# A new order table for the steps and the first loads of a windowed-attention and highway kernel

## The chip, the cores and the metric

The kernel runs on one core of a Trainium2 chip. The metric is the device time of one execution in microseconds (us). The engines of a core run side by side, each through its own program in order: PE (TensorE, matrix multiplies and transposes), DVE (VectorE), ACT (ScalarE), POOL (GpSimd) and SP (SyncE). They wait for one another on semaphores. Most loads are issued by POOL, the stores by SP.

## The reference

For each of 4 x 8 heads, 768 queries of 64 elements attend to the first 4 keys (the sinks) and to the last 128 keys. The result, 3072 tokens of 512 elements, goes through a highway layer.

```python
keep = (pos[None, :] < n_sink) | ((rel >= 0) & (rel < window))
a = softmax(where(keep, scale * q @ k.T, -1e9))
x = a @ v                                   # heads side by side: 3072 x 512
H = maximum(x @ w_h, 0.0)
T = 1.0 / (1.0 + exp(-(x @ w_t + b_t)))
out = T * H + (1.0 - T) * x
```

## The kernel before

The 3072 tokens are cut into 24 blocks of 128, six to a batch entry. The keys and values are cut into chunks that lie 64 rows off, so that a block needs chunks n-1, n and n+1. For each block n the work is a chain of small steps, and one step is one function. The steps are named as in the table ORDER (line 594):

- On PE, **Tq:n** and **Tk:n** (line 272) transpose the block's queries and the chunk's keys, eight small transposes each. From block 3 on they sit inside S ("hosted", line 528): S:n transposes the queries of a later block and the keys of another. Then ACT copies the result out of PSUM, **tq:n** and **tk:n** (line 283). The variants tqV and tkV do the copy on DVE.
- **S:n** (line 540, PE) makes the scores; **x0_:n** and **x1_:n** (line 339, ACT) take the exponentials of four heads each; **m0_:n** and **m1_:n** (line 347, DVE) multiply by the window's mask.
- **sk:n** (line 300, PE) and **es:n** (line 309, ACT) do the scores and exponentials of the sinks. They use a sink matrix that POOL copies for later batch entries (line 289, with tk:6, tk:12 and tk:18), and the sinks' values, a product with a small mask bm: fc:0 and fd:0 on DVE for the first batch entry, POOL for the others. POOL makes bm itself, with the two selections at lines 194 and 197.
- **A:n** (lines 354 and 366, PE) multiplies with the values. It needs value chunks n-1 to n+1, both masked halves of the exponentials, and, from block 1, the sinks. Placing A:n also places the loads of queries n+8 and of keys and values n+9 in POOL's program (do_A, line 560).
- **xh:n** (lines 390 and 396, DVE) divides by the sum; **X:n** (line 406, PE) transposes the result; **xT:n** (line 415) copies it on ACT, or xTV:n on DVE.
- The highway part: **Mh:n** and **Mt:n** (PE, lines 435 and 421) multiply with the two weights; **u:n** (ACT) takes a tanh; **d:n**, **e:n** and **o:n** (DVE) combine them; o:n also issues the store on SP.
- **wA:n** is a spare matmul of zeros into the buffer of A:n. It does no work for the result.

The scores have two PSUM buffers, the output of A one pair of banks (so A:n+1 waits for the copy xT:n), and sk, Mh and Mt share two buffers. Five xh and three each of u, d and e can be alive.

The order is written out by hand: the table lists all steps, and each engine runs its own steps in the table's order (line 629). Whatever an engine cannot yet do holds everything behind it on that engine. The loads of the first blocks stand in a list of their own at the head of POOL's program (lines 186 to 214). The very first loads (q0, k0, k1, v0, v1) come over SP and ACT in 32 bits.

Of the kernel before, what the change touches and what calls it, by code (L numbers as in the profile page):

```python
# [20 lines left out]
def kernel(  # L21
# [21 lines left out]
    B, H, S, D = q.shape  # L43
# [37 lines left out]
    def chunk_parts(n):  # L81
        b, c = divmod(n, NSC)
        if c:
            return [(slice(0, P), b, c * P - HP)]
        return ([(slice(0, HP), b - 1, S - HP)] if b else []) + ([(slice(HP, P), b, 0)] if b < B else [])

    def load_q(n):
        b, c = divmod(n, NSC)
        qsd = sd_pool.tile([P, H, D], FP16, tag="qsd", name="qsd")
        nc.gpsimd.dma_start(out=qsd, in_=q[b, :, c * P:(c + 1) * P, :].transpose([1, 0, 2]))  # L90
        q_sd[n] = qsd

    def load_k(n):
        ksd = sd_pool.tile([P, H, D], FP16, tag="ksd", name="ksd")
        for rows, b, s0 in chunk_parts(n):
            nr = rows.stop - rows.start
            nc.gpsimd.dma_start(out=ksd[rows], in_=k[b, :, s0:s0 + nr, :].transpose([1, 0, 2]))  # L97
        k_sd[n] = ksd

    def load_v(n):  # L100
        vt = v_ring[n % NV][:, 0:H * 65].rearrange("p (h e) -> p h e", e=65)
        for rows, b, s0 in chunk_parts(n):
            nr = rows.stop - rows.start
            nc.gpsimd.dma_start(out=vt[rows, :, 0:D], in_=v[b, :, s0:s0 + nr, :].transpose([1, 0, 2]))  # L104
# [12 lines left out]
    wh_sb = const.tile([P, NOC, DM], FP16, tag="wh")  # L117
# [25 lines left out]
    def load_f32(kind, n, eng):  # L143
        t = kf_first if (kind, n) == ("k", 0) else const.tile([P, H, D], FP32, tag=f"{kind}f{n}",
                                                              name=f"{kind}f{n}")
        src = {"q": q, "k": k, "v": v}[kind]
        for rows, b, s0 in ([(slice(0, P), 0, n * P)] if kind == "q" else chunk_parts(n)):
            nr = rows.stop - rows.start
            eng.dma_start(out=t[rows], in_=src[b, :, s0:s0 + nr, :].transpose([1, 0, 2]))
        {"q": q_sd, "k": k_sd, "v": vf_of}[kind][n] = t  # L150
# [6 lines left out]
    def tri(t, rows, lo, hi, base, step, cm):  # L157
        nc.gpsimd.affine_select(
            out=t[rows, lo:hi], in_=t[rows, lo:hi], compare_op=ALU.is_ge, fill=0.0,
            base=base, pattern=[[step, hi - lo]], channel_multiplier=cm)  # L160
# [6 lines left out]
    def load_w(w, sb):  # L167
        nc.gpsimd.dma_start(out=sb, in_=w.rearrange("(kc p) of -> p kc of", p=P))

    with tc.manual_schedule(engines={ENG.Pool, ENG.SP}):  # L170
        load_f32("q", 0, nc.sync)
        load_f32("k", 0, nc.scalar)
        load_f32("k", 1, nc.sync)
        load_f32("v", 0, nc.scalar)
        load_f32("v", 1, nc.sync)
        nc.sync.dma_start(out=bt32, in_=moe_b_t.unsqueeze(0))
        for b in range(B):
            nc.sync.dma_start(out=vs_dn[b], in_=v[b, :, 0:NSINK, :])
        nc.gpsimd.affine_select(
            out=ident, in_=ident, compare_op=ALU.is_equal, fill=0.0,  # L180
            base=0, pattern=[[-1, P]], channel_multiplier=1)
        tri(mask, slice(0, HP), 0, P, HP - 1, -1, 1)
        tri(mask, slice(HP, P), 0, P, 0, 1, -1)
        tri(mask, slice(0, HP), P, EW, 0, 1, -1)
        tri(mask, slice(HP, P), P, EW, -1, -1, 1)
        load_q(3)
        load_k(2)
        load_q(4)
        load_q(1)
        load_k(3)  # L190
        load_q(2)
        load_v(2)
        load_k(5)
        nc.gpsimd.affine_select(
            out=bm, in_=bm, compare_op=ALU.is_ge, fill=0.0,
            base=0, pattern=[[-NSINK, H]], channel_multiplier=1)
        nc.gpsimd.affine_select(
            out=bm, in_=bm, compare_op=ALU.is_ge, fill=0.0,
            base=NSINK - 1, pattern=[[NSINK, H]], channel_multiplier=-1)
        load_k(4)  # L200
        load_v(3)
        load_w(moe_w_h, wh_sb)
        load_q(5)
        load_k(6)
        load_w(moe_w_t, wt_sb)
        load_v(4)
        load_q(6)
        load_k(7)
        load_v(5)
        load_k(8)  # L210
        load_q(7)
        load_v(6)
        load_v(8)
        load_v(7)
# [378 lines left out]
    }  # L593
    ORDER = """
    mz0_:0 ma:0 na:0 Tq:0 na:1 Tk:0 tq:0 mz1_:0 tk:0 ma:1 wA:0 wA:0 Tk:1 mc:0 cv:0 tk:1 fa:0
    wA:0 wA:0 wA:0 S:0 cv:1 x0_:0 fb:0 x1_:0 wA:0 wA:0 wA:0 wA:0 Tq:3 m0_:0 tq:3 wA:0 Tk:2 m1_:0
    tk:2 fc:0 fd:0 wA:0 wA:0 wA:0 wA:0 wA:0 Tq:1 A:0 tq:1 S:1 xh:0 sk:1 x0_:1 x1_:1 Tq:2 m0_:1
    X:0 sk:3 xTV:0 es:1 Tk:3 m1_:1 tq:2 tk:3 wA:1 A:1 es:3 S:2 xh:1 x0_:2 x1_:2 Tk:4 m0_:2 sk:2
    tkV:4 X:1 es:2 m1_:2 S:3 xT:1 A:2 x0_:3 Mh:1 x1_:3 xh:2 tq:4 d:1 X:2 Mh:0 xT:2 m0_:3 tk:5
    m1_:3 Mh:2 d:0 S:4 d:2 Mt:0 x0_:4 x1_:4 m0_:4 A:3 u:0 m1_:4 Mt:1 tq:5 xh:3 tk:6 sk:4 e:0 u:1  # L600
    S:5 es:4 o:0 X:3 x0_:5 sk:5 xTV:3 e:1 A:4 x1_:5 m0_:5 Mt:2 tq:6 xh:4 tk:7 es:5 m1_:5 X:4 u:2
    S:6 xTV:4 o:1 A:5 x0_:6 e:2 Mh:3 x1_:6 xh:5 Mh:4 tq:7 m0_:6 tk:8 m1_:6 X:5 S:7 d:3 xT:5 d:4
    A:6 x0_:7 o:2 Mh:5 x1_:7 xh:6 Mt:3 tq:8 d:5 tk:9 X:6 m0_:7 u:3 Mt:5 m1_:7 xT:6 e:3 sk:7 u:5
    o:3 Tq:9 es:7 Mt:6 e:5 tq:9 o:5 u:6 S:8 A:7 x0_:8 Mh:6 x1_:8 xh:7 tq:10 m0_:8 X:7 tk:10
    m1_:8 sk:9 xT:7 d:6 S:9 es:9 e:6 A:8 x0_:9 o:6 Mt:7 x1_:9 xh:8 tq:11 Mt:4 m0_:9 tk:11 m1_:9
    u:7 X:8 u:4 S:10 xTV:8 e:4 A:9 x0_:10 o:4 Mh:8 x1_:10 xh:9 Mh:7 tq:12 m0_:10 tk:12 m1_:10
    X:9 S:11 xT:9 d:8 A:10 d:7 x0_:11 sk:11 e:7 x1_:11 Mt:8 xh:10 es:11 tq:13 Mh:9 o:7 tk:13 u:8
    m0_:11 X:10 S:12 xT:10 m1_:11 d:9 A:11 x0_:12 e:8 Mt:9 x1_:12 xh:11 tq:14 Mh:10 m0_:12 tk:14
    m1_:12 u:9 X:11 d:10 S:13 xT:11 o:8 A:12 x0_:13 e:9 sk:13 x1_:13 xh:12 Mt:10 es:13 m0_:13
    tq:15 Mh:11 m1_:13 tk:15 o:9 u:10 X:12 S:14 d:11 xT:12 e:10 A:13 x0_:14 o:10 Mt:11 x1_:14  # L610
    xh:13 tq:16 Mh:12 tk:16 m0_:14 u:11 m1_:14 X:13 S:15 d:12 xT:13 e:11 A:14 x0_:15 o:11 sk:15
    x1_:15 Mt:12 xh:14 es:15 tq:17 m0_:15 Mh:13 tk:17 m1_:15 u:12 X:14 d:13 S:16 xT:14 e:12 A:15
    x0_:16 o:12 Mt:13 x1_:16 xh:15 tq:18 Mh:14 m0_:16 tk:18 m1_:16 u:13 X:15 d:14 S:17 xT:15
    e:13 A:16 x0_:17 o:13 sk:17 x1_:17 Mt:14 xh:16 es:17 tq:19 m0_:17 Mh:15 tk:19 m1_:17 u:14
    X:16 d:15 S:18 xT:16 e:14 A:17 x0_:18 o:14 Mt:15 x1_:18 xh:17 tq:20 Mh:16 m0_:18 tk:20
    m1_:18 u:15 X:17 d:16 S:19 xT:17 e:15 A:18 x0_:19 o:15 sk:19 x1_:19 Mt:16 xh:18 es:19 m0_:19
    tq:21 Mh:17 m1_:19 tk:21 u:16 X:18 d:17 S:20 xT:18 e:16 A:19 x0_:20 o:16 Mt:17 x1_:20 xh:19
    tq:22 Mh:18 m0_:20 u:17 m1_:20 tk:22 sk:21 d:18 X:19 es:21 S:21 xTV:19 e:17 A:20 x0_:21 o:17
    Mt:18 x1_:21 xh:20 tq:23 Mh:19 m0_:21 u:18 m1_:21 tk:23 X:20 d:19 sk:23 xT:20 S:22 e:18
    es:23 A:21 x1_:22 o:18 Mt:19 x0_:22 xh:21 tk:24 m0_:22 X:21 xT:21 m1_:22 S:23 u:19 A:22  # L620
    x0_:23 e:19 Mh:20 xh:22 x1_:23 Mh:21 d:20 m0_:23 X:22 Mt:21 xT:22 m1_:23 d:21 A:23 o:19 u:21
    e:21 Mh:22 xh:23 Mt:22 d:22 o:21 X:23 u:22 Mt:20 xT:23 e:22 Tb:23 o:22 u:20 Ta:23 ub:23 e:20
    Ha:23 ua:23 o:20 Hb:23 da:23 db:23 ea:23 eb:23 pa:23 pb:23
    """

    with tc.manual_schedule(engines={ENG.PE, ENG.DVE, ENG.Activation, ENG.SP, ENG.Pool}):
# [40 lines left out]
```

The softmax here doesn't subtract the row's maximum and nothing guards it: scores larger than these inputs give would overflow.

## Time and profile before

| | |
|---|---|
| median of 3 runs | 124.67 us (123.35 to 126.68) |
| the profiled execution's own time | 122.54 us |
| its span, first to last instruction | 120.5 us |
| PE busy | 109.2 us (91%) |
| DVE busy | 103.1 us (86%) |
| ACT busy | 92.7 us (77%) |
| POOL busy | 73.7 us (61%) |
| granted TensorE clock | 0.996 |

The profile is of one execution. "L426" is line 426 of the kernel. In a timeline, a line gives start, duration, engine, line, operation, result and source, how many instructions are merged, and in brackets how long the engine was idle before it and what ended that. In a table of stretches, each number is the busy time of an engine in the stretch, with its count of instructions. A load on POOL shows the time POOL needs to issue it; when the data lands is a separate number of the transfer view. PE instructions overlap, so the step times in this text are the distances between starts.

### The profile page before, as it was taken

To read this page: it belongs to the slowest core of one execution; us is meant where nothing else is said; L and a number is where in the kernel's file an instruction comes from. 1 tells how busy PE (TensorE), PEld (TensorE's weight loads), DVE (VectorE), ACT (ScalarE), POOL (GpSimd) and SP (SyncE) were. 2 spreads that over 40 slices of the span, in tenths; PEclk is the share of its full clock that TensorE was granted. 3 is DMA by queue.
4 is the path that set the end of the run, shared out by engine and by line. 5 is a ranking of instruction groups with operands and counts; after the bars stand their busy time and mean duration, and the time that the engine had idled before them with its cause. 6 is when DMAs were issued, how large, how long until landed. Compare 5 with 4: busy or idle time off the path is not lost.

```text
span 120.5 us, 4964 instructions
## 1 busy us (share of the span) xinstructions
PE 109.2 (91%) x2105; PEld 66.0 (55%) x2105; DVE 103.1 (86%) x237; ACT 92.7 (77%) x155; POOL 73.7 (61%) x97
## 2 busy tenths in 40 slices
PE   5999696999999999997999999989999999999920
PEld 1443565456666466565567656645775676545610
DVE  6889456769999979998889999899998999899990
ACT  2258478949987879998799999979999979961610
POOL 5999996958799999999899999760000000000000
PEclk9999999999999999999999999999999999999998
DMA  2999999999999999999999999999122202202242
GB/s 67 218 172 151 151 172 170 189 155 146 134 196 203 170 235 193 152 201 195 165 201 109 191 200 202 200 163 234 29 92 87 95 5 87 87 5 87 87 174 87
DMA packets 79847, 17.65 MB, mean 146 GB/s; under 512 B 75601, under 2 KB 76881, under 8 KB 79826
## 3 DMA queue, kind: packets, MB, share of 16 engines
q0 software_dynamic: 71888, 9.97, 131.5%
q1 hardware_dynamic: 6882, 7.11, 18.8%
q10 hardware_dynamic: 1056, 0.26, 1.3%
q8 instruction: 16, 0.26, 0.9%
q14 instruction: 5, 0.04, 0.1%
HBM read 21.01 MB, written 6.29 MB: 227 GB/s over the span
## 4 chain that ended last, share of the span: by engine, by line
PE 57%; DMA 18%; POOL 7%; DVE 6%; issue 4%; ACT 4%; DVEq 0%; ACTq 0%; POOLq 0%
DMA qsd<-in_q_dram 18%; PE tps L426 11%; PE hps L439 11%; PE av L368 6%; PE av L379 5%; PE sps L336 4%; PE sps L323 4%; PE sps L280 4%; PE sk L305 3%; PE tps L424 3%; ACT e L341 3%; PE av L385 3%; PE av L412 3%; POOL qsd L90 2%; POOL ksd L97 2%
## 5 line engine op out<-in xcount | busy, mean ns | idle before, releaser
L341 ACT ACTIVATE e<-sps,ebias 128x768 f16<-128x768 f32 x48 | 40.7, 898 | 8.4 <-PE sps L336 7.0
L349 DVE TENSOR_TENSOR e<-e,mask 128x768 f16<-128x768 f16 x48 | 24.8, 550 | 2.4 <-ACT e L341 2.4
L285 ACT COPY t<-sps 128x512 f16<-128x512 f16 x45 | 24.4, 586 | 1.5 <-PE sps L280 1.5
L104 POOL DMA_DIRECT2D v<-in_v_dram x26 | 22.4, 861 | 3.6 <-DVE e L349 1.0
L426 PE MATMUL tps<-wt_sb,xT 128*128 128x512 f16 x92 | 23.6, 379 | 0.0
L439 PE MATMUL hps<-wh_sb,xT 128*128 128x512 f16 x92 | 23.0, 379 | 0.0
L97 POOL DMA_DIRECT2D ksd<-in_k_dram x26 | 22.5, 874 | 0.2
L90 POOL DMA_DIRECT2D qsd<-in_q_dram x23 | 21.5, 936 | 1.3 <-DMA qsd<-in_q_dram 0.8
L451 DVE SCALAR_TENSOR_TENSOR ee<-u,dd 128x512 f16<-128x512 f16 x23 | 17.2, 748 | 0.9 <-ACT u L432 0.7
L398 DVE TENSOR_TENSOR xh<-av,rec 128x512 f16<-128x512 f32 x24 | 16.6, 691 | 0.8
L432 ACT ACTIVATE u<-tps 128x512 f16<-128x512 f32 x23 | 13.8, 602 | 4.3 <-PE tps L426 4.2
L445 DVE SCALAR_TENSOR_TENSOR dd<-hps,xh 128x512 f16<-128x512 f32 x23 | 15.6, 687 | 1.5 <-PE hps L439 1.1
L457 DVE SCALAR_TENSOR_TENSOR otok<-xh,ee 128x512 f32<-128x512 f16 x23 | 15.8, 689 | 0.6
L439 PEld LDWEIGHTS <-xT 128*128 128x128 f16 x92 | 8.9, 98 | 9.2 <-ACT xT L417 0.2
L426 PEld LDWEIGHTS <-xT 128*128 128x128 f16 x92 | 9.0, 98 | 8.6
L417 ACT COPY xT<-av 128x512 f16<-128x512 f16 x19 | 11.2, 587 | 2.1 <-PE av L412 2.0
L323 PE MATMUL sps<-t,t 64*128 64x128 f16 x192 | 11.9, 217 | 0.1
L368 PEld LDWEIGHTS <-e 64*64 64x64 f16 x384 | 9.3, 107 | 3.0 <-issue 1.2
L368 PE MATMUL av<-v,e 64*64 64x66 f16 x384 | 10.8, 193 | 0.2 <-DVE xT L417 0.2
L379 PE MATMUL av<-v,e 128*128 128x66 f16 x192 | 10.4, 195 | 0.0
L393 DVE RECIPROCAL rec<-av 128x8 f32<-128x8 f32 x24 | 4.9, 204 | 5.9 <-PE av L385 4.4
L336 PE MATMUL sps<-t,t 64*64 64x64 f16 x384 | 8.0, 198 | 1.4 <-issue 1.4
(79 smaller groups left out, 140.4 us busy)
## 6 DMA issues: line engine op xcount, KB each, us to landing
out_dram<-otok SPq DMA_DIRECT2D x23, 256.0 KB, 5.1
qsd<-in_q_dram POOLq DMA_DIRECT2D x23, 128.0 KB, 6.7
ksd<-in_k_dram POOLq DMA_DIRECT2D x19, 128.0 KB, 6.6
v<-in_v_dram POOLq DMA_DIRECT2D x19, 128.0 KB, 6.8
wh_sb<-in_moe_w_h_dram POOLq DMA_DIRECT2D x1, 512.0 KB, 7.0
wt_sb<-in_moe_w_t_dram POOLq DMA_DIRECT2D x1, 512.0 KB, 8.3
ksd<-in_k_dram POOLq DMA_DIRECT2D x7, 64.0 KB, 6.6
v<-in_v_dram POOLq DMA_DIRECT2D x7, 64.0 KB, 6.1
```

The lines of the kernel that those rows point to most:

```text
L90: nc.gpsimd.dma_start(out=qsd, in_=q[b, :, c * P:(c + 1) * P, :].transpose([1, 0, 2]))
L97: nc.gpsimd.dma_start(out=ksd[rows], in_=k[b, :, s0:s0 + nr, :].transpose([1, 0, 2]))
L104: nc.gpsimd.dma_start(out=vt[rows, :, 0:D], in_=v[b, :, s0:s0 + nr, :].transpose([1, 0, 2]))
L285: (eng or nc.scalar.copy)(out=t.rearrange("p a (h b) -> p h a b", b=HP), in_=t_view(s_tile(n, g), isinstance(n, tuple) and n[1:] in F32_T))
L323: nc.tensor.matmul(sps[:, hh, hl * EW:hl * EW + P], lhsT=kT[n][rows, hp, :], rhs=qT[n][rows, hp, :], start=True, stop=True)
L341: nc.scalar.activation(out=e.rearrange("p a b c -> p a (b c)"), in_=s_tile(n, g)[:, :, 0:2 * EW], func=AF.Exp, bias=ebias, scale=SCALE)
L349: nc.vector.tensor_tensor(out=ev, in0=ev, in1=m.unsqueeze(1).to_broadcast([P, 4, EW]), op=ALU.mult)
L368: nc.tensor.matmul(av[part, h // 4, h % 4, 0:_AVN], lhsT=e_at(n, h)[src, P:EW], rhs=vt[src, 65 * h:65 * h + _AVN], start=(h % 4 == 0), sto ...
L398: nc.vector.tensor_tensor(out=xh.rearrange("p (h d) -> p h d", d=D), in0=av_of.pop(n)[:, :, 0:D], in1=rec_of.pop(n).unsqueeze(2).to_broadc ...
L426: nc.tensor.matmul(tps, lhsT=xT[:, kc, :], rhs=wt_sb[:, kc, :], start=False, stop=(kc == NOC - 1))
L439: nc.tensor.matmul(hps, lhsT=xT[:, kc, :], rhs=wh_sb[:, kc, :], start=(kc == 0), stop=(kc == NOC - 1))
L451: nc.vector.scalar_tensor_tensor(out=ee, in0=u_of.pop(n), scalar=1.0, in1=dd_of.pop(n), op0=ALU.add, op1=ALU.mult)
```

## The change

Nothing is added to or taken from what is computed. The first loads in POOL's program come in another order, and the two selections that make bm come after the load of q5. In the table, the steps of blocks 0 to 13 and of the last five blocks come in another order. In the middle the rows are the same, shifted. Block 1's keys and queries are transposed ahead of those of block 3; the first highway step comes after A:2 for block 0, and Mh:1 only before S:8. Three copies of transposes are on DVE (tkV:3, tqV:2, tqV:3) where there was one (tkV:4), and the copies xTV are at blocks 1, 4, 6, 12 and 20 (0, 3, 4, 8 and 19 before). There are 20 spares where there were 16.

```diff
@@ -183,32 +183,32 @@
-        load_q(3)
         load_k(2)
-        load_q(4)
         load_q(1)
         load_k(3)
         load_q(2)
+        load_k(5)
+        load_k(4)
+        load_q(4)
+        load_k(6)
+        load_v(3)
+        load_q(3)
         load_v(2)
-        load_k(5)
+        load_v(4)
+        load_w(moe_w_h, wh_sb)
+        load_q(5)
         nc.gpsimd.affine_select(
             out=bm, in_=bm, compare_op=ALU.is_ge, fill=0.0,
             base=0, pattern=[[-NSINK, H]], channel_multiplier=1)
         nc.gpsimd.affine_select(
             out=bm, in_=bm, compare_op=ALU.is_ge, fill=0.0,
             base=NSINK - 1, pattern=[[NSINK, H]], channel_multiplier=-1)
-        load_k(4)
-        load_v(3)
-        load_w(moe_w_h, wh_sb)
-        load_q(5)
-        load_k(6)
         load_w(moe_w_t, wt_sb)
-        load_v(4)
         load_q(6)
         load_k(7)
         load_v(5)
+        load_q(7)
         load_k(8)
-        load_q(7)
         load_v(6)
@@ -593,34 +593,34 @@
-    wA:0 wA:0 wA:0 S:0 cv:1 x0_:0 fb:0 x1_:0 wA:0 wA:0 wA:0 wA:0 Tq:3 m0_:0 tq:3 wA:0 Tk:2 m1_:0
-    tk:2 fc:0 fd:0 wA:0 wA:0 wA:0 wA:0 wA:0 Tq:1 A:0 tq:1 S:1 xh:0 sk:1 x0_:1 x1_:1 Tq:2 m0_:1
-    X:0 sk:3 xTV:0 es:1 Tk:3 m1_:1 tq:2 tk:3 wA:1 A:1 es:3 S:2 xh:1 x0_:2 x1_:2 Tk:4 m0_:2 sk:2
-    tkV:4 X:1 es:2 m1_:2 S:3 xT:1 A:2 x0_:3 Mh:1 x1_:3 xh:2 tq:4 d:1 X:2 Mh:0 xT:2 m0_:3 tk:5
-    m1_:3 Mh:2 d:0 S:4 d:2 Mt:0 x0_:4 x1_:4 m0_:4 A:3 u:0 m1_:4 Mt:1 tq:5 xh:3 tk:6 sk:4 e:0 u:1
...
+    wA:0 wA:0 wA:0 S:0 cv:1 x0_:0 fb:0 x1_:0 wA:0 wA:0 wA:0 wA:0 Tk:2 m0_:0 tk:2 wA:0 Tq:1 m1_:0
+    tq:1 wA:0 wA:0 wA:0 S:1 x0_:1 x1_:1 wA:0 wA:0 wA:0 wA:0 Tk:3 m0_:1 tkV:3 wA:0 Tk:4 m1_:1
+    Tq:2 tk:4 A:0 tqV:2 S:2 xh:0 x0_:2 fc:0 X:0 sk:2 sk:1 xT:0 fd:0 es:1 x1_:2 Tq:3 m0_:2 tqV:3
+    es:2 m1_:2 wA:1 wA:1 A:1 S:3 xh:1 x0_:3 X:1 sk:3 xTV:1 es:3 A:2 m0_:3 tq:4 x1_:3 Mh:0 xh:2
+    tk:5 sk:4 d:0 X:2 es:4 S:4 xT:2 m1_:3 Mh:2 x0_:4 x1_:4 m0_:4 A:3 d:2 tq:5 Mt:0 xh:3 tk:6
+    sk:5 m1_:4 u:0 X:3 S:5 xT:3 e:0 es:5 A:4 x0_:5 o:0 Mt:1 x1_:5 m0_:5 xh:4 tq:6 Mt:2 tk:7
+    m1_:5 u:1 X:4 u:2 S:6 xTV:4 e:2 A:5 x0_:6 o:2 Mh:3 x1_:6 xh:5 tq:7 Mh:4 m0_:6 tk:8 m1_:6 X:5
+    S:7 d:3 xT:5 d:4 A:6 x0_:7 Mh:5 xh:6 x1_:7 Mt:5 d:5 tq:8 tk:9 m0_:7 Mt:3 u:5 m1_:7 e:5 Mh:1
+    u:3 o:5 Tq:9 d:1 X:6 tq:9 sk:7 xTV:6 e:1 es:7 S:8 e:3 A:7 x0_:8 o:1 Mt:6 o:3 x1_:8 xh:7
+    tq:10 Mh:6 tk:10 m0_:8 u:6 m1_:8 X:7 S:9 xT:7 d:6 A:8 x0_:9 e:6 Mt:4 o:6 x1_:9 xh:8 tq:11
+    Mt:7 tk:11 m0_:9 u:4 m1_:9 X:8 u:7 S:10 e:4 xT:8 o:4 sk:9 x0_:10 Mh:8 es:9 m0_:10 x1_:10 A:9
+    d:8 tq:12 m1_:10 sk:11 tk:12 Mh:7 xh:9 es:11 d:7 X:9 S:11 xT:9 e:7 A:10 x0_:11 o:7 Mt:8
...
+    d:20 S:23 xT:21 e:18 sk:23 x0_:23 A:22 o:18 es:23 x1_:23 Mt:21 xh:22 m0_:23 X:22 u:21 Mh:21
+    m1_:23 xT:22 A:23 d:21 e:21 Mh:22 xh:23 Mt:22 d:22 X:23 o:21 u:22 Mt:20 xT:23 e:22 Tb:23
+    o:22 u:20 Ta:23 ub:23 e:20 Ha:23 ua:23 o:20 Hb:23 da:23 db:23 ea:23 eb:23 pa:23 pb:23
```

More of the change, by code (lines that the diff above doesn't have):

```diff
@@ L601 @@
[L601 to L623, printed above, removed]
+    wA:0 wA:0 wA:0 S:0 cv:1 x0_:0 fb:0 x1_:0 wA:0 wA:0 wA:0 wA:0 Tk:2 m0_:0 tk:2 wA:0 Tq:1 m1_:0
@@ new lines @@
+    S:7 d:3 xT:5 d:4 A:6 x0_:7 Mh:5 xh:6 x1_:7 Mt:5 d:5 tq:8 tk:9 m0_:7 Mt:3 u:5 m1_:7 e:5 Mh:1
[3 more added lines that the diff above has]
+    d:8 tq:12 m1_:10 sk:11 tk:12 Mh:7 xh:9 es:11 d:7 X:9 S:11 xT:9 e:7 A:10 x0_:11 o:7 Mt:8
+    x1_:11 xh:10 tq:13 Mh:9 m0_:11 tk:13 m1_:11 u:8 X:10 d:9 S:12 xT:10 e:8 A:11 x0_:12 o:8 Mt:9
@@ new lines @@
+    x1_:12 xh:11 tq:14 Mh:10 m0_:12 tk:14 m1_:12 u:9 X:11 d:10 S:13 xT:11 e:9 A:12 x0_:13 o:9
+    Mh:11 x1_:13 xh:12 Mt:10 tq:15 d:11 tk:15 m0_:13 sk:13 u:10 m1_:13 X:12 es:13 S:14 xTV:12
+    e:10 A:13 x0_:14 o:10 Mt:11 x1_:14 xh:13 tq:16 Mh:12 m0_:14 tk:16 m1_:14 u:11 X:13 d:12 S:15
+    xT:13 e:11 A:14 x0_:15 o:11 sk:15 x1_:15 xh:14 Mt:12 es:15 m0_:15 tq:17 Mh:13 m1_:15 tk:17
+    u:12 X:14 d:13 S:16 xT:14 e:12 A:15 x0_:16 o:12 Mt:13 x1_:16 xh:15 tq:18 Mh:14 m0_:16 tk:18
+    m1_:16 u:13 X:15 d:14 S:17 xT:15 e:13 A:16 x0_:17 o:13 sk:17 x1_:17 Mt:14 xh:16 es:17 m0_:17
@@ new lines @@
+    tq:19 Mh:15 m1_:17 tk:19 u:14 X:16 d:15 S:18 xT:16 e:14 A:17 x0_:18 o:14 Mt:15 x1_:18 xh:17
+    tq:20 Mh:16 m0_:18 tk:20 m1_:18 u:15 X:17 d:16 S:19 xT:17 e:15 A:18 x0_:19 o:15 sk:19 x1_:19
+    Mt:16 xh:18 es:19 m0_:19 tq:21 Mh:17 m1_:19 tk:21 u:16 X:18 d:17 S:20 xT:18 e:16 A:19 x0_:20
+    o:16 Mt:17 x1_:20 xh:19 tq:22 Mh:18 m0_:20 tk:22 m1_:20 u:17 X:19 d:18 S:21 xT:19 e:17 A:20
+    x0_:21 o:17 Mt:19 x1_:21 xh:20 tq:23 Mh:19 m0_:21 u:19 m1_:21 tk:23 sk:21 d:19 X:20 es:21
+    S:22 xTV:20 e:19 A:21 x1_:22 o:19 Mt:18 x0_:22 xh:21 tk:24 Mh:20 m0_:22 u:18 m1_:22 X:21
```

## The prediction

> **What bounds the kernel now.** I read the page's totals first, then the stretches, then the waits and the first 20 us of each engine's timeline.
>
> ```profile
> span 120.5 us, 4964 instructions
> PE 109.2 (91%) x2105; PEld 66.0 (55%) x2105; DVE 103.1 (86%) x237; ACT 92.7 (77%) x155; POOL 73.7 (61%) x97
> PE 57%; DMA 18%; POOL 7%; DVE 6%; issue 4%; ACT 4%; DVEq 0%; ACTq 0%; POOLq 0%
> ```
>
> PE leads, and the chain that ended last is PE plus the transfers of the start. The stretches say where. Columns are the stretch, then busy us of PE, PEld, DVE, ACT and POOL, clock, DMA share, GB/s:
>
> ```profile
> 9.78:19.35 9.57, 7.22 (x170) 4.75 (x170) 5.96 (x15) 6.57 (x12) 9.32 (x13) 1.00 2.34 160
> 19.35:33.64 14.29, 13.94 (x315) 8.77 (x311) 11.35 (x24) 11.96 (x21) 10.95 (x14) 1.00 2.54 160
> 33.64:44.32 10.68, 10.50 (x206) 5.87 (x199) 10.45 (x18) 8.95 (x15) 10.49 (x14) 1.00 2.16 198
> 44.32:56.86 12.54, 11.53 (x286) 7.37 (x279) 11.09 (x22) 11.57 (x20) 12.54 (x15) 1.00 2.03 186
> 56.86:104.68 47.82, 47.20 (x994) 29.78 (x993) 44.42 (x84) 44.09 (x76) 21.87 (x29) 1.00 1.25 137
> ```
>
> From 19.35 us on PE idles 0.35, 0.18, 1.01 and 0.62 us in the four stretches; 0.84 and 0.54 of that are instruction-side pauses ("issue") that no order table moves. Idle time that could be won lies before 19.35 us: 2.35 us, and some 1.6 us of spare matmuls (seven of about 0.22) after 9.78. DVE is almost as full as PE between 33.64 and 44.32: 10.45 of 10.68 us. That matters below.
>
> The start runs at the pace of the loads. Each of the lines below is one transfer; PE's transpose of q1 starts just when it lands.
>
> ```profile
> 12.61 0.29 PE L280 MATMUL sps<-ident,qsd 64*128 64x64 f16 x8 [0.60 <-DMA qsd<-in_q_dram]
> 13.91 0.32 PE L336 MATMUL sps<-t,t 64*64 64x64 f16 x16
> 16.51 0.50 PE L368 MATMUL av<-v,e 64*64 64x66 f16 x16
> 10.06 0.24 POOL L194 TENSOR_SCALAR_AFFINE_SELECT bm<-bm 128x8 f16<-128x8 f16 x1
> 10.37 1.20 POOL L197 TENSOR_SCALAR_AFFINE_SELECT bm<-bm 128x8 f16<-128x8 f16 x1
> 20.85 0.88 POOL L104 DMA_DIRECT2D v<-in_v_dram  x1 [1.01 <-DVE e L349]
> 24.85 0.69 POOL L104 DMA_DIRECT2D v<-in_v_dram  x1 [0.69 <-DMA wt_sb<-in_moe_w_t_dram]
> ```
>
> The DMA view, asked for one issue at a time, gives start plus time to landing: q3 9.06, k2 10.5, q4 11.4, q1 12.4, k3 13.5, q2 14.3, v2 15.4, k5 16.2, k4 17.3, v3 18.3, wh 20.3, q5 21.2, k6 22.1, wt 24.5, v4 25.6, q6 26.5, k7 27.4. From q3 to v3 that is one load per 1.03 us, although POOL issues one per 0.89. So **a load's place in the queue sets its landing**: place 1 at 9.06, 2 at 10.5, 3 at 11.4, then about 1.0 each. POOL also never has more than eight loads outstanding: v5 is issued at 20.85 after wh lands (20.3), the second half of v6 at 24.85 after wt (24.5), and each time eight are in flight. The "DVE e" that the first wait names had long been done.
>
> **What the Trainium skill says.** "DMA: Bandwidth & Descriptors", section "Why small descriptors are slow (HBM only)": every packet has a fixed cost on top of its bytes. The trace agrees: 75601 of 79847 packets are under 512 B, and a 128 KB load takes 1.03 us of the stream. The same page, "Anatomy of one DMA — SWDGE (gpsimd) path": the engines don't wait on semaphores, the issuing sequencer does. Here that is POOL, so what is behind a held load in POOL's program waits too (1.01 us at 20.85). "TensorE: Matmul & The Clock Gate", section "Architectural detail: the array is 16× 32×32, not 1× 128×128": ACT and DVE are strict first-in-first-out, and PE pulls only weight loads forward. The trace shows no step overtaking another.
>
> **The change, part by part.**
>
> *Loads.* The same loads and bytes, in new places: k2, q1, k3, q2, k5, k4, q4, k6, v3, q3, v2, v4, wh, q5, wt. By the places above: k2 9.06, q1 10.5, k3 11.4, q2 12.4, k5 13.4, k4 14.3, q4 15.4, k6 16.3, v3 17.3, **q3 18.3, v2 19.3**, v4 20.3, wh 22.3, q5 23.2, wt 25.5. From q6 on the stream is as before, so later blocks gain nothing from it. Early S steps gain: q1 comes two places sooner. q3 is 9 us later and v2 4 us later.
>
> *The two bm selections* (0.24 + 1.20 us, last end 11.57 now) move behind six more 128 KB loads (k4, k6 in two halves, v3, v4, q5) and wh. With eight outstanding, q5 waits for q4's landing (15.4), so it is issued about 15.8 to 16.7 and bm is ready at about 18.2. If nothing held POOL it would be 17.1; I take 18.2. Queued on DVE behind fc:0, which waits for it: fd:0, m0_:2, tqV:3, m1_:2, xh:1. PE needs fd:0 for A:1 and tqV:3 for S:3.
>
> *PE before 19.35.* S without transposes takes 0.58 us, a group of eight transposes 0.22, A:0 0.75, a pair of exponentials 1.69 (all from the timeline). S:0 is unchanged. Tk:2 at 9.8, Tq:1 at 10.5, both copies done at 11.46 as now, S:1 at 11.5 (13.58 before), its exponentials 12.2 to 13.9. Tk:3 at 13.1 and Tk:4, which waits for k4 and for a score buffer, at 14.3; Tq:2, then A:0 to 15.55, S:2 to 16.15, xh:0, X:0 to 16.8, sk:2 and sk:1 to 17.3. Then **Tq:3 waits for q3 until 18.3** and **A:1 for v2 until 19.35**; the spares in between (two of 0.22) cost nothing. At 19.35 the old order has done the same six transpose groups, S:1, S:2, A:0, X:0, two sk, and A:1 besides. The new one is behind by one A: 0.92 us. The head start of 2 us for S:1 is lost in these waits.
>
> *19.35 to S:6.* With S 0.81, A 0.92, Mh 0.86, Mt 1.08, X and sk 0.22 each, and 0.9 for rec and xh on DVE, the new row gives: A:1, S:3 to 21.1, X:1 21.7 (after xh:1, which DVE starts only at 20.6, behind fd:0 and m1_:2), A:2 23.05, S:4 25.2, A:3 26.95, S:5 29.3, A:4 30.2, S:6 done 33.4. The old one has S:6 done at 33.64 (the timeline) but also Mh:1. Behind by 0.86 - 0.24 = **0.6**. Putting the highway later lets S run with fewer waits, but PE was idle for only 0.35 us of this stretch, so that is all there was to win.
>
> *S:6 to X:7.* d:1, e:1, o:1 now come in this stretch, and the copy of xT:6 is put on DVE: 0.60 + 0.72 + 0.61 + 0.42 = 2.35 us more on an engine that has 0.23 us free. DVE was free for xh:7 at 44.4, so it now is at about 44.4 - 0.2 (it enters the stretch ahead) + 2.35 = 46.6. X:7 follows 0.95 later, at 47.5; the old X:7 is at 46.37 with the same steps done. PE waits about 0.6 us there, behind Mh:6. **Behind by 1.15.** That is the "one block behind": the cover for xh:7 is two highway steps (1.94 us), and the DVE row is longer.
>
> *Blocks 8 to 10.* A:9 is put before d:8 and m1_:10 are through on DVE, so X:9 waits about 0.2 us. Behind by 1.3.
>
> *Blocks 11 to 19* have the same row as now, step for step from about S:14, and PE stays full: 0. *End:* S:23 comes one Mh later, sk:23 moves behind it, of the PE steps after that only Mh:21 and Mt:21 change places; A:23 may wait 0.1 to 0.2 us for xT:22. Below zero is excluded, PE being full there. I take 0. *Spares:* four more, 0.9 us, all ahead of a wait that is longer: 0; without that cover 0.9. *Other queues:* the loads that A steps issue keep their order on POOL, with tk:6's sink copies at the same place between them; SP's stores follow the o steps (0, 2, 5, 1, 3), and SP is idle for most of the time between stores now: 0. *Copies on DVE* in block 2 and 3 (0.42 instead of 0.57 us on ACT): inside the same waits, 0.
>
> Sum: +0.92 - 0.3 + 0.55 + 0.15 = **+1.3 us** on the profiled execution, whose own time is 122.54 (span 120.5 and 2.04 around it): 123.8. The median of the runs, 124.67, is 2.1 above the profiled one, so I put the forecast on the median: **126.0**.
>
> **Rivals.**
> *The early S chain pays.* If POOL isn't held at eight and its 1.5 us of selections no longer leave a hole in the issue, bm is ready at 17.1, fd:0 at 18.0, and v2 might land with it. A:1 at 18.1 is 1.25 us sooner: 124.67 + 1.3 - 1.25 = 124.7, or 124.2 if DVE also comes through block 7 without the 0.55. Against it: the stream, not POOL, sets landings from 9 to 18 us. A gain over 2% would need nearly all of the 2.35 us of early idle time; nothing supports that.
> *bm decides (slower).* POOL's program holds the selections behind q5. A:1 is ready 0.95 us after bm, S:3 1.85 us after. At 18.2 both are just covered by v2 and A:1; from about 18.4 on every us is a us of PE time. If q5 and the loads before it are held longer, so that bm is ready at 20.0, the cost is 1.6 more: 127.6. For it: the waits at 20.85 and 24.85 show that such holds are real and up to 1 us each. Against: POOL shows no hold before 20 us now.
>
> **Numbers.** Forecast 0.50 (own range 124.7 to 127.3), early chain pays 0.15, bm decides 0.35. Runs of this kernel spread from 123.35 to 126.68, so 2%, 2.5 us, is about what a measurement can tell from no change. Over 2% slower (127.2): 0.30 of the rival's 0.35, 0.08 of the forecast's: 0.38. Over 2% faster (122.2): 0.05. Within: 0.57. The range goes from 123.7, half of the early-chain case, to 129.0, a bm at 21 us or DVE holding X:7 and X:9 for twice what I worked out.
>
> **What would show it.** Right: S:1 near 11.5; a DMA wait of PE before Tq:3 (18.3) and at A:1 (19.3); S:6 done near 33.4; DVE with no gap up to xh:7 near 46.6, PE waiting at X:7; blocks 12 to 20 of about 4 us as now. Wrong: A:1 before 18.5 (loads land sooner than their places say), fc:0 past 19 (bm decides), X:7 before 46.4, or new waits after block 11.

## The result and the profile after

The changed kernel takes 127.99 us (median of 4 runs, 127.4 to 128.6) where the kernel before takes 124.53 (median of 4). The ratio is 1.031, with a 95% interval of 1.021 to 1.041: slower. Medians here and below are of all runs; a ratio is of the means of those runs of each kernel that lie within 1.5% of its fastest, since some runs fall in a slower state. The profiled execution's span is 125.5 us, 5.0 more than before.

The page's totals of the changed kernel:

```profile
span 125.5 us, 4972 instructions
PE 109.2 (87%) x2109; PEld 66.2 (53%) x2109; DVE 103.5 (82%) x239; ACT 92.0 (73%) x153; POOL 71.0 (57%) x97
PE 58%; DVE 22%; issue 7%; DMA 5%; ACT 4%; POOL 1%; DVEq 0%; ACTq 0%
```

PE's busy time is the same to 0.1 us, so PE is idle 5 us longer. In the chain, "issue" (PE waits for nothing that the profile shows) grew from 4% to 7% of the span and DVE from 6% to 22%; transfers fell from 18% to 5%. The stretches, with the columns as in the prediction; the second ends with S:6, as it does before, the later ones end at other steps than before (the third at X:7):

```profile
9.78:19.35 9.57, 6.75 (x139) 3.78 (x139) 6.33 (x16) 6.25 (x11) 8.20 (x13) 1.00 2.79 153
19.35:35.86 16.51, 14.17 (x342) 9.40 (x343) 10.66 (x22) 11.42 (x21) 13.19 (x16) 1.00 2.40 166
35.86:49.71 13.85, 12.63 (x223) 7.29 (x218) 12.15 (x24) 10.77 (x18) 13.43 (x19) 1.00 2.04 163
49.71:64.05 14.34, 12.06 (x261) 7.73 (x261) 11.70 (x23) 11.93 (x21) 12.01 (x17) 1.00 2.09 201
64.05:109.90 45.85, 45.01 (x956) 28.32 (x954) 42.95 (x81) 41.43 (x70) 15.65 (x20) 1.00 1.00 119
```

PE's idle time in them is 2.82, 2.34, 1.22, 2.28 and 0.84 us. Only the first is near what it was. Nearly all of the rest is not waiting for any engine or load. These are all the pauses of PE from 20 us on whose bracket is 0.5 us or more; the bracket is idle time and what ended it:

```profile
25.54 0.20 PE L280 MATMUL sps<-ident,ksd 64*128 64x64 f16 x2 [0.54 <-issue]
32.19 0.35 PE L379 MATMUL av<-v,e 128*128 128x66 f16 x6 [1.29 <-issue]
40.20 0.21 PE L280 MATMUL sps<-ident,ksd 64*128 64x64 f16 x2 [1.22 <-issue]
61.50 0.26 PE L336 MATMUL sps<-t,t 64*64 64x64 f16 x8 [2.11 <-issue]
79.46 0.27 PE L305 MATMUL sk<-t,ks 128*128 128x128 f16 x2 [0.84 <-issue]
```

Together 6.0 us. The same list of the kernel before has two lines, 1.4 us:

```profile
56.31 0.19 PE L336 MATMUL sps<-t,t 64*64 64x64 f16 x1 [0.84 <-issue]
81.13 0.28 PE L336 MATMUL sps<-t,t 64*64 64x64 f16 x10 [0.54 <-issue]
```

Each pause falls in the middle of a group that has no reason to stop: after six of eight transposes, after two of eight matmuls, after 15 of 16. That speaks against a wait written in the program. So I counted PE's instructions in the trace: weight loads, matmuls, and the 44 to 47 semaphore and drain instructions between them. The pauses come at instructions 705, 961, 1217, 1985 and 2753 after, and 1985 and 3009 before. All are 193 plus a multiple of 256. The page also has a queue that I had not looked at, the same in both kernels:

```profile
q8 instruction: 16, 0.26, 0.9%
```

Sixteen packets and 0.26 MB, 16 KB each: PE's program, 4254 instructions before, fetched in **pieces of 256**. Every pause ends 1.3 to 1.8 us after such a packet has ended. The Trainium skill has this in "Runtime: NRT & Kernel Launch", section "Instruction fetch mechanics": blocks of 16 KiB, 256 instructions, fetched over a queue of the engine's own, the cost "mostly hidden". The size agrees with the trace. "Mostly hidden" holds for most boundaries; at five of them the changed kernel stands for 7.0 us in all.

For a few pieces, from the trace: how long PE takes to run the piece, how long after entering it the fetch of the next one begins, and the distance of the two starts across the boundary (it holds some 0.2 us of work that the bracket leaves out).

| PE instructions | before: run / fetch after / stop | after: run / fetch after / stop |
|---|---|---|
| 449 to 705 | 7.13 / 3.57 / 0 | 5.20 / 3.56 / 0.73 |
| 705 to 961 | 5.78 / 2.86 / 0.07 | 5.17 / 3.51 / 1.48 |
| 961 to 1217 | 5.80 / 3.62 / 0.30 | 6.60 / 5.39 / 1.41 |
| 1729 to 1985 | 4.27 / 2.92 / 1.04 | 5.31 / 5.23 / 2.30 |
| 2497 to 2753 | 5.84 / 3.73 / 0.21 | 5.17 / 3.85 / 1.06 |
| 2753 to 3009 | 6.01 / 4.26 / 0.73 | 6.71 / 2.81 / 0 |
| 3521 to 3777, no loads left | 4.95 / 0.43 / 0.03 | 4.99 / 0.72 / 0 |

Where PE stops, it goes on 2.4 to 3.1 us after the fetch has begun (about 1 us of transfer and 1.3 to 1.8 more). While loads run, the fetch mostly begins 2 to 5.4 us after PE enters the piece (sooner in three pieces of these two kernels, 0.6 to 1.9); when they have ended, within 0.8 us (once 1.6).

So two things make a stop: PE is through its 256 instructions soon, or the fetch begins late. The stops at 705 and 2753, 1.8 us, go with the first. The new order puts the highway later, and eight instructions of Mh take 0.86 us where as many small ones of A or S take about 0.1. In the piece up to 705 there are 4 long matmuls where there were 12, PE also waits 0.7 us less in it, and **PE gets to its end sooner**: 5.2 us instead of 7.1. At 961, 1.5 us, both are there: PE is 0.6 us sooner, the fetch 0.65 later. The stops at 1217 and 1985, 3.7 us, are of the second kind. There PE takes longer than before (6.60 us for 5.80, 5.31 for 4.27) and stops longer all the same, because **the fetch begins 1.8 and 2.3 us later**. Why it does is not shown. Four spares more move every boundary by eight instructions besides.

### The profile page after: what moved, and what is told of

It reads as the page before. It is cut to its first block, busy times and chain, and to the rows that moved or that the text cites. A ratio compares the mean times of both kernels' runs of the same rounds, so it can differ in the third digit from the quotient of the medians.

```text
span 125.5 us, 4972 instructions
## 1 busy us (share of the span) xinstructions
PE 109.2 (87%) x2109; PEld 66.2 (53%) x2109; DVE 103.5 (82%) x239; ACT 92.0 (73%) x153; POOL 71.0 (57%) x97
## 4 chain that ended last, share of the span: by engine, by line
PE 58%; DVE 22%; issue 7%; DMA 5%; ACT 4%; POOL 1%; DVEq 0%; ACTq 0%
PE hps L439 13%; PE tps L426 12%; PE av L368 6%; PE av L379 6%; DMA v<-in_v_dram 5%; PE sps L336 4%; PE av L412 4%; DVE otok L457 3%; PE sps L280 3%; PE av L385 3%; PE sps L323 3%; PE tps L424 3%; DVE ee L451 3%; DVE e L349 3%; PE sk L305 2%
## 5 line engine op out<-in xcount | busy, mean ns | idle before, releaser
L285 ACT COPY t<-sps 128x512 f16<-128x512 f16 x43 | 23.2, 584 | 2.3 <-PE sps L280 2.3
L439 PE MATMUL hps<-wh_sb,xT 128*128 128x512 f16 x92 | 23.5, 379 | 0.0
L451 DVE SCALAR_TENSOR_TENSOR ee<-u,dd 128x512 f16<-128x512 f16 x23 | 16.4, 715 | 0.7 <-ACT u L432 0.2
```

What stands on the lines that cost most here:

```text
L285: (eng or nc.scalar.copy)(out=t.rearrange("p a (h b) -> p h a b", b=HP), in_=t_view(s_tile(n, g), isinstance(n, tuple) and n[1:] in F32_T))
L439: nc.tensor.matmul(hps, lhsT=xT[:, kc, :], rhs=wh_sb[:, kc, :], start=(kc == 0), stop=(kc == NOC - 1))
L451: nc.vector.scalar_tensor_tensor(out=ee, in0=u_of.pop(n), scalar=1.0, in1=dd_of.pop(n), op0=ALU.add, op1=ALU.mult)
```

## The experiments

Two theories. *Pieces:* the time comes from stops at the end of pieces of PE's program. *Order:* it comes from the waits of my forecast. The kernel before ran again beside each group of experiments; its median lies between 123.48 and 124.95. Code is shortened. Stops below are distances of starts across a boundary, over 0.45 us, as in the table: 1.77 us before, 6.98 after, in the profiled executions.

**1. The changed kernel, 144 PE instructions more.** Nothing but zeros in the warm-up. It shifts all boundaries.

```diff
-        warm_up(8)
+        warm_up(4)     # and 76 more, inside:
+        for _ in range(76):
+            nc.tensor.matmul(w[0:32, 0:32], lhsT=warm[:, 0:32], rhs=warm[:, 0:32], start=True, stop=True)
```

> The changed kernel with 72 more tiny matmuls of zeros (32 columns) among the warm-up matmuls and four long ones fewer, so that PE's program is 144 instructions longer ahead of all real work; nothing else differs. Theory 'pieces': the trace of the changed kernel shows PE's program fetched in pieces of 16 KB, 256 instructions; PE stops at instructions 705, 961, 1217, 1985 and 2753 (all 193 plus a multiple of 256) until a piece is there, 7.0 us in all, against 1.8 us at 1985 and 3009 before. Then the stops must move: PE stops again at 193 plus multiples of 256, which are now other steps. By the lengths of the pieces in the trace, three instead of five would be too short: 125.0 to 126.5 us. Theory 'order' (the steps of my forecast: A:1 waits for its values, DVE is behind at X:7): the waits are at the same steps as in the changed kernel, 127.5 to 128.5 us.

Measured: 124.46 us beside 124.95 of the kernel before (ratio 0.995, 0.988 to 1.003), lower than either theory had said. Work was added, and 3.5 us less came out than in the changed kernel: all that the change had lost. The five stops are gone, and there are two elsewhere (I had expected three), at 2497 and 3009, again 193 plus multiples of 256. They sum to 3.3 us, 3.7 less than in the changed kernel; the profiled span is 2.7 us shorter:

```profile
66.14 0.32 PE L372 MATMUL av<-v,e 64*64 64x66 f16 x9 [1.35 <-issue]
79.77 0.22 PE L340 MATMUL sps<-t,t 64*64 64x64 f16 x3 [1.55 <-issue]
```

**2. The kernel before, 80 PE instructions more.**

```diff
-        warm_up(8)
+        warm_up(5)     # and 43 small ones as above
```

> The kernel before with 40 more tiny matmuls of zeros and three long ones fewer in the warm-up: 80 PE instructions more, same table, same loads. Theory 'pieces': the boundaries now fall so that six pieces instead of two are run through in under 5 us; more stops at 193 plus multiples of 256, 126.5 to 128.5 us, as slow as the changed kernel with nothing of the change in it. Theory 'order': 124 to 125 us, no new stop.

Measured: 125.27 beside 124.95 (1.002, 0.994 to 1.010). My expectation missed. The stops did move, to 705 and 2241, and sum to 3.8 us instead of 1.8 in the profiled execution, but not to six, and the median doesn't show them. Three pieces that PE ran through in 4.5 to 4.8 us had no stop, since their fetches began 0.6 to 1.0 us after PE entered the piece; two others, of 4.6 and 4.8 us, with fetches 4.1 and 4.3 us after, did stop. The length of a piece alone doesn't foretell a stop; the fetch's delay varies too much. Since before has stops in some places as well, its luck and that of this kernel are about the same.

**3 and 4. No loads late.** Queries from block 11 on and keys from chunk 12 on are one tile, values from chunk 13 on are stale, so part of the output is not computed. PE, ACT and DVE run the same steps.

```diff
     def load_set(n):
-        if on(n):
-            load_q(n); load_k(n + 1); load_v(n + 1)
+        if on(n):
+            if n < 11: load_q(n); load_k(n + 1)
+            else: q_sd[n], k_sd[n + 1] = same_q, same_k   # loaded once, at 11
+            if n < 12: load_v(n + 1)
```

> The changed kernel without most loads from block 11 on: queries and keys from there on are all one tile, values from block 13 on are the old ones, so that part of the output is left wrong; the steps of PE, ACT and DVE are the same. No load runs after about 45 us. Theory 'pieces', and that loads in flight delay the fetch: after 45 us the fetch begins within 1 us of PE's entering a piece (2.2 to 5.2 us in the changed kernel), the stops at 1985 (2.3 us) and 2753 (1.1 us) go, 124.3 to 125.0 us. Theory 'order': no change beyond 45 us, 127.5 to 128.5.

> The kernel before without the same loads (again part of the output is left wrong). Theory 'pieces': its two stops (1.0 and 0.7 us) go, 122.5 to 123.2 us, and the distance to the changed kernel without these loads is under 2 us. Theory 'order': distance as between the full kernels, 3.5 us.

Measured: 124.63 for the changed one, 121.45 for the one before, beside 124.95. No stop is left after 45 us in either; fetches begin within 1.2 us of PE's entering the piece, often ahead of it. The changed kernel keeps its early three, which lie where loads still run:

```profile
25.62 0.20 PE L282 MATMUL sps<-ident,ksd 64*128 64x64 f16 x2 [0.48 <-issue]
32.81 0.36 PE L381 MATMUL av<-v,e 128*128 128x66 f16 x6 [1.83 <-issue]
41.10 0.21 PE L282 MATMUL sps<-ident,ksd 64*128 64x64 f16 x2 [1.49 <-issue]
```

So the loads delay the fetch. The distance of 3.2 us between the two, which I had put under 2, is these three stops: I had not counted them. Without them the profiled spans are 118.8 (123.2 less 4.4) for the changed one and 118.9, with no stop at all, for the one before. The kernel before came out below its expected range: it gained 3.5 us in the median, although its profiled execution has only 1.8 us of stops. That execution was 2 us faster than the median of its runs. Whether the others stop longer, or the late loads cost something else too, is not shown.

The early stops come again wherever the early part of the program is the same. At 705 and 961 together the changed order stops for 2.2 us in the changed kernel, 2.7 here and 2.6 in experiment 11; the order before stops for at most 0.1 in the kernel before, here and in experiment 9.

**5, 6, 7. Fewer loads outstanding.** POOL reads one element of the fifth (fourth) load back ahead of each load.

```diff
+    def gate(ap):               # called ahead of each load
+        if len(issued) >= CAP:      # 5 or 4
+            nc.gpsimd.tensor_copy(out=gate_to[64:65], in_=issued[-CAP])
+        issued.append(ap)
```

> The changed kernel with a one-element copy on POOL ahead of each load, which reads what the fifth load back brought, so that at most five loads are outstanding instead of eight. Theory 'pieces' (a fetch of PE's program waits behind the loads in flight): with five eighths of the queue the fetch begins 1.4 to 3.4 us after PE enters a piece instead of 2.0 to 5.4, a piece is there 3.8 to 5.8 us after, and the five stops of 7.0 us shrink to under 2 us: 123 to 124.5 us. If the delay doesn't depend on how many loads are queued, the stops stay and POOL has some 70 copies more: 128 us or more.

> The kernel before with the same limit of five loads. Theory 'pieces': its 1.8 us of stops go, 123.0 to 124.2 us where the kernel before has 124.5 to 125, if the start keeps its pace (a load per 1.03 us). Against it: if the copies and the shorter queue slow the loads of the start, up to 1 us more, 125.5.

> The kernel before with at most four loads outstanding. Theory 'pieces': fetches begin within 2.7 us, no stops; the stream is just kept busy (four loads of about 1 us against a delay of some 4 us), so the start may lose up to 1 us: 122.5 to 124.5 us.

Measured: 131.2, 130.77 and 140.49, beside 123.48. The stops are gone with five (0 in both kernels) and 0.5 us with four; most fetches begin within 2.5 us, and a load lands in about 5.0 and 4.4 us instead of 6.7. That part of the theory held. The time did not: the loads of the start fall behind, and with them POOL's sink copies. The profiled clock was lower as well, 0.94 to 0.96 instead of 0.996; what share of the loss is the clock's was not separated. Of the kernel before with five outstanding, the waits:

```profile
DVE rec L406 <- PE av L398: 11.3, 4, 8.7
PE sk L318 <- POOL ks L307: 5.7, 1, 5.7
```

One wait for the sink copy of 5.7 us, where PE waits 0.6 us for it in the kernel before. Here the fetch was made sooner at the price of late loads, and the start had no slack for that.

**8. The changed table with q3 and v2 early.** The order of the first loads on POOL, in short:

```diff
-        k2 q1 k3 q2 k5 k4 q4 k6 v3 q3 v2 v4 wh q5 bm wt
+        k2 q1 k3 q2 k4 q3 v2 bm q4 k5 v3 k6 v4 wh q5 wt
```

> The changed kernel with its first loads in the order k2, q1, k3, q2, k4, q3, v2, then the two selections of bm, q4, k5, v3, k6, v4, wh, q5, wt: q3 lands near 14.3 and v2 near 15.4 us instead of 18.3 and 19.3. The table is the changed one. My step on the start (A:1 waits for v2, 0.92 us): A:1 starts at 17.6 to 18.3 us instead of 19.45, 1.2 us less in the end, 126.5 to 127.2 us, with the same stops. Theory 'pieces' alone: what is won at the start is lost again where PE comes to the end of a piece sooner than the fetch, 127.5 to 128.5 us.

Measured: 127.3 beside 123.48 (1.024, 1.017 to 1.032), an interval that overlaps the changed kernel's. A:1 starts at 18.20 instead of 19.45 and X:3 at 28.08 instead of 29.28. This version has six stops, 6.0 us in all, which is less than the 7.0 of the changed kernel, so they alone don't take the 1.2 us back. In this profile the granted clock also fell to a half from 32.0 to 35.4 us, so its later stretches can't be compared. Inconclusive: what was won at the start can't be followed to the end.

**9, 10, 11. Late loads paced by their buffers.** Queries from block 13 on and keys from chunk 14 on are in pools of three, so POOL can't run ahead and fill the queue.

```diff
-        qsd = sd_pool.tile([P, H, D], FP16, tag="qsd", name="qsd")
+        qsd = (sd_pool if n < 13 else late_pool).tile([P, H, D], FP16, tag="qsd", name="qsd")   # bufs=3; keys alike
```

> The kernel before with the queries and keys from block 13 on in a pool of three buffers, so that POOL loads block n only when S:(n-5) has read its buffer: three loads per block instead of a full queue, from about 55 us on; landings are still two blocks ahead of their use. Theory 'pieces': fetches in that stretch begin within 1 to 2.5 us, the stop at 3009 goes, the one at 1985 may stay: 1 to 2 us less than before, 122.8 to 124.0. If POOL's sink copies now come too late, PE waits for them at sk:13 or sk:19: 125 to 127.

> The changed kernel with 144 more PE instructions in the warm-up and the same pacing. Its two stops with the 144 alone were at 2497 and 3009 (1.5 and 1.7 us, at 64 and 78 us): both should go, 121.5 to 123.0 us, which would be below the kernel before. If pacing doesn't shorten the fetch, 124.5.

> The changed kernel with the pacing alone. Theory 'pieces': the stops before 45 us stay (3.6 us), the one at 2753 (1.1 us) goes and the one at 1985 (2.3 us) shrinks: 125 to 127 us. Theory 'order': 127.5 to 128.5.

Measured: 127.99 (1.034), 125.39 (1.010) and 129.0 (1.042), beside 123.99. Again the late stops went (none after 62 us in any) and again more was lost; all three missed the range of theory 'pieces'. In the profile of the last the clock was also at a half from 32.9 to 36.3 us. POOL's copies for the sinks stand behind the held loads. Of the kernel before, paced:

```profile
PE sk L306 <- POOL ks L295: 5.4, 3, 2.9
69.73 0.62 PE L306 MATMUL sk<-t,ks 128*128 128x128 f16 x8 [2.92 <-POOL ks L295]
95.15 0.62 PE L306 MATMUL sk<-t,ks 128*128 128x128 f16 x8 [1.05 <-POOL ks L295]
```

This is the alternative that the first of these expectations names, at more than its price. The key of a load set is held one block longer than I had worked out with three buffers.

**12. The kernel before, 16 instructions more, paced with four buffers for keys.**

```diff
-        warm_up(8)
+        warm_up(7)     # and 9 small ones; queries in three late buffers, keys in four
```

> The kernel before with 16 PE instructions more in the warm-up and the pacing eased: queries from block 13 on in three buffers, keys from chunk 14 on in four, so that both are loaded when S:(n-5) is done, one block sooner than in the paced runs. With 16 more, the trace of before gives no piece shorter than 5.1 us (the shortest is 4.3 us now). Theory 'pieces': no stop over 0.5 us after 55 us, the sink copies come in time, 121.8 to 123.3 us, below the kernel before (124.0 to 125.0). If the sink copies are still late, PE waits for them and the time is 124 to 126.

Measured: 123.11 beside 123.96, the medians of 23 and 27 runs (ratio 0.993, 0.986 to 1.000, from the six and five fastest). The profile is of an execution of 124.73. No wait of PE for the sink copies is left among its larger ones, and no stop after 58 us. One stop of 2.2 us stays at 57.68, which I had not expected; its fetch began 5.0 us after PE entered the piece. Of the versions that compute the whole result it is the only one whose interval lies below 1, by 0.7% and just clear of no change; by the two ratios it is some 4% ahead of the changed one.

**What the order alone costs.** With the stops taken off, the starts of the same X step can be set side by side:

| | X:7 | X:9 | X:11 | last matmul ends |
|---|---|---|---|---|
| before (stops 1.77) | 46.37 | 54.48 | 62.42 | 113.42 |
| changed (6.98) | 46.09 | 54.83 | 62.44 | 113.21 |
| changed, 144 more (3.28; none before X:11) | 46.99 | 55.73 | 63.51 | 114.23 |

Where no stop comes early, the new order is behind by 0.62 at X:7 (0.2 of it may be v2, which held A:1 until 19.64 there and until 19.45 in the changed kernel), 1.25 at X:9 and 0.8 at the end. In the changed kernel nothing of this is seen: the 3.6 us of stops before X:7 make X:7 only 2.7 us later than in experiment 1 (49.71 for 46.99). The likely reason is that DVE and ACT catch up while PE stands. Of the 5.0 us between the two profiled spans, 5.2 are stops, and the order's own loss is hidden in them. Each figure is from one execution.

## Why the prediction was right or wrong

The sign and the range held (127.99 in 123.7 to 129.0). **The cause did not**, and the forecast of 1.3 us more was well short of the 3.5 measured. That it landed in the range was luck: it came through a mechanism that I had excluded.

- *"0.84 and 0.54 of that are instruction-side pauses ('issue') that no order table moves."* This is the step that failed. They are the ends of pieces of PE's program, and an order table moves them: it decides which instructions fill a piece, and each spare shifts all later boundaries. The stops grew from 1.8 to 7.0 us; I had put that at 0. Experiment 1 moved them with no change of the order, and the loss was gone. How an order makes a fetch begin later stays open.
- *Spares: 0.* In time, yes; in instructions, no.
- *Loads by place.* Right. PE waited for q3 until 18.52 (forecast 18.3); A:1 began when v2 landed, at 19.45 (19.35); the scores of S:1 began at 11.87 (11.5).

```profile
18.52 0.29 PE L280 MATMUL sps<-ident,qsd 64*128 64x64 f16 x8 [0.57 <-DMA qsd<-in_q_dram]
19.45 0.45 PE L368 MATMUL av<-v,e 64*64 64x66 f16 x16
17.39 0.25 DVE L248 TENSOR_SCALAR vs<-bm 32x8 f16<-32x8 f16 x2 [0.34 <-POOL bm L203]
11.39 0.89 POOL L104 DMA_DIRECT2D v<-in_v_dram  x1 [0.92 <-DVE e L349]
```

- *Eight outstanding.* POOL was held at the tenth issue, v3, until 11.39, although it had shown no hold that early before. This fits a limit of eight: the first load had landed, and the second, q1, let PE go on at 10.89. The DVE step that the bracket names touches no tile of this load. *bm at 18.2:* it was ready at 17.4, since the two selections took 0.19 us each instead of 1.44 together. The rival "bm decides", which names 127.6 us, is refuted: fc:0 waited 0.34 us, and fd:0 was done in time. That its number is near the measured one is chance.
- *S:6 done at 33.4.* Measured 35.86 with 2.2 us of stops, so 33.65 without. *X:7 at 47.5, 1.15 behind:* 49.71, and 46.09 without stops. DVE did run with no gap from 44.0 until xh:7 was done at 49.6, and the chain goes over it, but PE did not wait the 0.6 us at X:7. The loss is hidden there; it is 0.62 in experiment 1, about half of my step. DVE's two pairs of e and o took 1.28 us each, 0.64 apiece, where I had put 0.72 and 0.61.
- *Behind by 1.3 after block 10:* 1.25 at X:9 in experiment 1, 0.8 at the end. The sum for the order was right in kind, and at the end too large by half a us.
- *Blocks 11 to 19: 0.* Wrong by the same cause: stops of 2.30 and 1.06 us lie from 59 to 80 us, where before has 1.04 and 0.73.
- *New waits after block 11* were named as a sign that the prediction is wrong. They came, at 61.5 and 79.5 us.

## What to carry to other kernels

An "issue" pause in the middle of a group of like instructions is a reason to count. If the places of such pauses differ by multiples of 256 instructions, with the engine's semaphore instructions counted, and a packet of the instruction queue ends shortly before PE goes on (1.3 to 1.8 us here), the engine ran out of program, and every edit ahead of it, a spare included, can move it. Before an order is judged by its time, shift the boundaries with instructions that do nothing and see whether the difference stays.

A piece of many small instructions leaves little time for a late fetch: most stops here ended pieces of 4.3 to 5.4 us. But several of 6.0 to 6.9 us ended in a stop too, with fetches that began 4.3 to 5.8 us after PE had entered them, and three of 4.5 to 4.8 us did not, with fetches within 1 us. So long matmuls among the small ones may help; that was not tried. Thin out the loads only where nothing else is queued behind them on the issuing engine: experiments 5 to 7 and 9 to 11 lost more than they won.

## What was not expected of the hardware

PE's fetch of 16 KB of its own program takes about 1 us, but it mostly begins 2 to 5.4 us after PE has entered a piece while loads run, and 0.4 to 0.8 us after without. With four or five loads outstanding it was mostly 0.2 to 2.5. After a stop PE goes on 1.3 to 1.8 us after the end of the transfer. The delay differs between executions: for the changed kernel's piece from 961 to 1217 it was 5.39, 5.80 (experiment 3) and 5.20 us (experiment 11). This may be a part of the spread of the kernel before (123.35 to 126.68); that wasn't measured, nor why the fetch begins late, in the queue of the transfers or on PE's side.

In three profiled executions the granted clock fell to a half for 3.4 us, 0.2 to 1.5 us after the end of a stop: in experiment 8 (stop of 1.76 us, ended at 31.3 us), 11 (1.76, 32.7) and 12 (2.2, 57.7). These are their clock lines, one digit for a fortieth of the span, in tenths (9 is 90% or more):

```profile
PEclk9999999999589999999999999999999999999997
PEclk9999999999679999999999999999999999999996
PEclk9999999999999999999689999999999999999996
```

It did not fall after the stop of 2.3 us in the changed kernel, nor after those of 2.0 in experiments 2 and 3, and it fell in experiments 5 to 7 with no such stop before it. So whether a stop can bring it about is not shown. Half the clock for 3.4 us can cost PE 1.7 us, which is another reason not to read one profiled execution alone.
